# DeltaNet and maxout FFN on one core: beta over the expanded squared norm, the norm on GpSimd, halved transposes, and a PSUM source for the last unit

## The chip, the cores and the metric

The kernel runs on one core of a Trainium2 chip. A core has TensorE (PE in the profile, PEld for its weight loads), VectorE (DVE), ScalarE (ACT), GpSimd (POOL) and SyncE (SP), which only issues DMAs here. ScalarE and GpSimd can issue DMAs as well. Each engine works through its own list of instructions in order, and waits on semaphores for the others. The metric is the device time of one execution in microseconds.

## The reference, cut to what matters

```python
k_n = k / (np.linalg.norm(k, axis=-1, keepdims=True) + 1e-06)
state = np.zeros((B, H, D, D))                      # B, H, S, D = 4, 8, 768, 48
for t in range(S):
    kt, vt, bt = k_n[:, :, t], v[:, :, t], beta[:, :, t, None]
    y[:, :, t] = np.einsum('bhd,bhde->bhe', q[:, :, t], state)
    v_old = np.einsum('bhde,bhd->bhe', state, kt)
    state = state + bt[:, :, :, None] * np.einsum('bhd,bhe->bhde', kt, vt - v_old)
# then x = y as (3072, 384), and
h = np.maximum(np.maximum(x @ w1, x @ w2), x @ w3)  # w1..w3 (384, 768)
out = h @ w_out                                     # w_out (768, 384)
```

The keys stay unnormalised in the kernel. The norm n + 1e-6 enters in two places: beta / (n + 1e-6)^2 scales the key products, and the values are multiplied by n + 1e-6.

## The kernel before, in words

The 768 time steps are cut into 12 chunks of 64. Each chunk is two units (batches with g = 0 and g = 1), and four units make a group, so there are 6 groups (m = 0 to 5). For each unit the keys are transposed on TensorE (`turn`, tile p_t, L345) or with DVE transposes (`turn_blocks`, L396), the products of keys with keys are made (`gram`, p_g, L422) and copied to `at`, with keys against queries in `pt`.

Within a group, each 32 by 32 diagonal block of every unit and head is inverted on VectorE, one block per partition (`solve`). `solve` takes the diagonal of the products (the squared norms), makes the norm, beta over its square, scales the blocks (L560), and eliminates column by column (L574 and L578, two instructions per step). It is a generator: each `yield` ends a portion, and the schedule calls `some(solving, n)` to issue n more portions. For group 0 the blocks come through copies in on-chip memory (`to_blocks`, `first_blocks`), and the inverse goes back by a DVE transpose (L586) and copies (`placed`, L512) into `ut`. For the other groups both ways go through DRAM (`at_d`, `blocks`; `y_d`).

`norms_of` transposes the norms into `nrm`, and `scale` (L303) multiplies the loaded values v_t with them, on GpSimd for all chunks but the last two. Then come, for each chunk: the join of two blocks to 64 (z, j), the product of keys with the state (`old_k`, p_k, subtracted from v_t in L768), the new values (`new`, p_u, L784), the step of the state (`step`, p_s, L814), the output (`to_y`, p_y, L828) and its transpose into `xt`.

The FFN of a group runs while the recurrence of the next one is computed and the blocks of the group after that are solved. There is no automatic schedule: the order of the instructions is the order in which the Python code issues them. The main loop goes through the portions of `ffn(m)` and issues other work behind each: what `LINKS` names for group m + 1, then portions of `solve(m + 2)`:

```python
if i == 8:
    solving = solve(m + 2)
links(m + 1, late.get(m, LINKS).get(i, ""))
...
elif i > 7:
    some(solving, 3 if i > 8 else 1)
```

For m = 1 and 2 portion 8 in `LINKS` is "s0 y0 N2", portions 6 and 7 hold N0 and N1. N is `load_blocks(n)` for a later unit: two memsets and 16 DMA issues, all on GpSimd (L375, L380), since its default queue is GpSimd's. Portion 16 holds P0, a `scale` on GpSimd. In the loop of m = 3 there are no N loads for a group beyond the last.

At the start, loads go out by SP in a fixed order, `turn` and `gram` of the eight first units follow, `solving` is advanced by 1 and then by 17 portions for group 0, and weights are unpacked by ScalarE, VectorE and GpSimd in turn (`weights`, L255 to L270) from pieces that `fetch` loads (w_bits).

Of the kernel before, what the change touches and what calls it, by code (L numbers as in the profile page):

```python
# [14 lines left out]
ALU = mybir.AluOpType  # L15
# [3 lines left out]
BL = 32  # L19
HB = 16  # L20
# [3 lines left out]
def kernel(  # L24
# [31 lines left out]
    nc = tc.nc  # L56

    B, H, S, D = q.shape
# [83 lines left out]
    def load_q(n, queues=one_queue):  # L142
        load(q, qpad[n % NQ], n, queues)
# [128 lines left out]
        )  # L272


    def norm(out, ksum, root, t):

        nc.scalar.sqrt(root, ksum)
        nc.vector.tensor_scalar_max(t, root, 1e-30)
        nc.vector.reciprocal(t, t)
        nc.vector.tensor_tensor(out=t, in0=t, in1=ksum, op=ALU.mult)  # L280
        nc.vector.tensor_tensor(out=t, in0=t, in1=root, op=ALU.add)
        nc.vector.tensor_scalar(
            out=out, in0=t, scalar1=0.5, scalar2=1e-6, op0=ALU.mult, op1=ALU.add
        )

    def small(name, *shape):
        one = name[-1] == "0" or name[-2:] == "bl" or name == "warm"
        return work.tile([128, *shape], FP32, name=name, bufs=2 - one)
# [3 lines left out]
    def norms_of(m, bl):  # L292
        for cc in range(2):
            t = small("nrm", 48)
            for bb in range(2):
                at = 16 * (1 - bb)
                nc.vector.transpose(
                    out=t[rows(bb), at : at + BL], in_=bl[rows(cc)]
                )
            nrms[2 * m + cc] = t[:, 16:32].rearrange("p (g h) -> p g h", g=2)  # L300
# [14 lines left out]
    bl_0 = []  # L315

    def first_norms():
        nc.vector.transpose(out=nrm_0.rearrange("p c g h -> p (c g h)"), in_=bl_0[0])


    kqts, ats, pts, xs, at_d = {}, {}, {}, {}, {}
# [1 line left out]
    def square(name):  # L323
        return work.tile([128, H, C], FP32, name=name, tag="square", bufs=17)

    def by_par(t):
        return t.rearrange("p (j two) x -> p two j x", two=2)
# [83 lines left out]
    def gram(n, parts=(0, 1), queues=one_queue, copy=nc.scalar.copy, later=False):  # L411
        kqt, g = kqts[n], n % 2
        p_g = ps_two("p_g")

        whole = len(parts) == 2 and not g
        for j in range(NP):
            for par in range(2):
                for bb in range(2):
                    kq = kqt[dims(par), j, bb ^ g]
                    for i in (0,) if whole else parts:  # L420
                        c0 = j * 128 + i * C
                        nc.tensor.matmul(  # L422
                            p_g[
                                rows(bb ^ (g * i)), par, c0 : c0 + C * (1 + whole)
                            ],
                            kq[:, 0],
                            kq if whole else kq[:, i],
                        )
        p_v = p_g.rearrange("p two (j i t) -> p two j i t", j=NP, i=2)
        if 1 in parts:  # L430
            pt = pts[n] = square("pt")
            if later:
                return lambda: copy(by_par(pt), p_v[:, :, :, 1])
            else:
                masked(pt, p_v[:, :, :, 1])
        if 0 not in parts:
            return
        at = ats[n] = square("at")
        copy(by_par(at), p_v[:, :, :, 0])  # L439
        if queues:  # L440
            to_dram(n, queues)
# [17 lines left out]
    def in_rows(t):  # L459
        return t.rearrange("p s r -> p (s r)")[:, 0 : BL * BL].rearrange(  # L460
            "p (j i) -> p j i", i=BL
        )
# [5 lines left out]
            "p (s r) -> p s r", s=2  # L468
        )

    def to_blocks(n, engines):


        cc, g = divmod(n, 2)
        for i, engine in enumerate(engines):
            bb, half = divmod(i, 2)
            r, x0 = block(bb, half), 16 * cc + 8 * g
            to = in_rows(in_wo(0))[r, x0 : x0 + H]
            of = ats[n][r, :, BL * half : BL * (half + 1)]
            if engine is nc.scalar:  # L480
                engine.copy(to, of)
            else:
                engine.tensor_copy(to, of)
# [18 lines left out]
        )  # L502


    def placed(cc, i, copy=nc.vector.tensor_copy, xs_of=slice(0, 2 * H)):
        bb, half = divmod(i, 2)
        r = block(bb, half)
        to = ut[cc][r, :, :, BL * half : BL * (half + 1)].rearrange(
            "p g h i -> p (g h) i"
        )  # L510
        of = in_rows(xs[0])[r, :, 16 * cc : 16 * (cc + 1)].rearrange("p i x -> p x i")
        copy(to[:, xs_of], of[:, xs_of])  # L512

    def solve(m):


        x = in_rows(xs[m])
# [7 lines left out]
            nc.gpsimd.memset(y_bl, 0.0)  # L525
        elif m > 2:
            nc.scalar.copy(y, zero.to_broadcast(y.shape))
        bl = small("bl", BL)
        norm(bl, diagonal(x), small("root_bl", BL), small("nt_bl", BL))
        if m == 1:  # L530
            y = ps_two("y_p").rearrange("p b (j i) -> p (b j) i", i=BL)
            nc.scalar.copy(y, zero.to_broadcast(y.shape))
        if m == 2:
            yield
        if m:
            norms_of(m, bl)
            if m == 2:
                yield
            nc.vector.reciprocal(bl, bl)
        else:  # L540
            bl_0.append(bl)
            bl = small("inv_bl", BL)
            nc.vector.reciprocal(bl, bl_0[0])
        nc.vector.tensor_tensor(out=bl, in0=bl, in1=bl, op=ALU.mult)
        nc.vector.tensor_tensor(out=bl, in0=bl, in1=beta_bl[:, m] if m else beta_0, op=ALU.mult)
        if m > 2:
            nc.scalar.copy(diagonal(y), bl)
        else:
            (nc.vector if m == 1 else nc.gpsimd).tensor_copy(diagonal(y), bl)
        if m < FINE:  # L550
            size, xv, yv = HB, in_blocks(xs[m]), in_blocks(y_bl)
            xb = xv[:, :, :, 0:HB]
            by = bl.rearrange("p (s i) -> p s i", i=HB)[:, :, None, :]
            by = by.to_broadcast([128, 2, HB, HB])
        else:
            size, xv, yv = BL, x[:, None], y[:, None]
            xb, by = x, bl[:, None, :].to_broadcast([128, BL, BL])
# [2 lines left out]
        nc.vector.tensor_tensor(out=xb, in0=xb, in1=by, op=ALU.mult)  # L560
        yield
        for j in range(size - 1):
            a, b = j + 1, size - 1 - j
            n = BL // size
            tmp = work.tile([128, 256], FP32, name="tmp", bufs=1)
            t_v = tmp[:, 0 : n * a * b].rearrange("p (s c i) -> p s c i", s=n, i=b)
            row, column, rest = (
                xv[:, :, j, None, j + 1 : size],
                yv[:, :, 0:a, j, None],
                yv[:, :, 0:a, j + 1 : size],  # L570
            )
            if n == 1:
                row, column, rest, t_v = (t[:, 0] for t in (row, column, rest, t_v))
            nc.vector.tensor_tensor(  # L574
                out=t_v, in0=row.to_broadcast(t_v.shape),
                in1=column.to_broadcast(t_v.shape), op=ALU.mult,
            )
            nc.vector.tensor_tensor(out=rest, in0=rest, in1=t_v, op=ALU.subtract)  # L578
            if m == 1 and j == BL - 8:
                nc.scalar.copy(done[:, :, 0:HB], y[:, :, 0:HB])  # L580
            elif m == 1 and j == BL - 2:
                nc.vector.tensor_copy(done[:, :, HB:BL], y[:, :, HB:BL])
            yield
        if m == 0:
            back = in_rows(xs[0])
            nc.vector.transpose(out=back, in_=y.rearrange("p c i -> p i c"))  # L586
            yield
            for i in range(4):
                if i % 2:
                    n = H * (i == 3)  # L590
                    if n:
                        placed(0, i, nc.vector.tensor_copy, slice(0, n))
                    placed(0, i, nc.scalar.copy, slice(n, 2 * H))
                else:
                    placed(0, i, nc.vector.tensor_copy)
            return
        y_d = dram.tile([2, 2, B, H, BL, BL], FP32, name="y_d")
        for cc in range(2):
# [22 lines left out]
    def diagonal(t):  # L621
        return t.rearrange("p j i -> p (j i)")[:, 0 : BL * BL : BL + 1]
# [714 lines left out]
    def keys(n, queues=one_queue, copy=nc.scalar.copy):  # L1337
        gram(n, (0,), queues, copy)
# [5 lines left out]
    load_q(0)  # L1344
    load_k(7)
    load_q(1)
    for _ in range(2):
        fetch(nc.sync)
    load_v(0)
    fetch(nc.sync)  # L1350
    busy(6, ident)
    turn(0, (0,))
    turn(1, (0,), nc.vector.tensor_copy)
    A, V, P = nc.scalar, nc.vector, nc.gpsimd
    keys(0, None)
    to_blocks(0, (P, P, P, P))
    turn(2, (0,))
    keys(1, None, nc.vector.tensor_copy)
    to_blocks(1, (V, V, V, P))
    turn(3, (0,))  # L1360
    keys(2, None)
    to_blocks(2, (A, P, A, P))
    keys(3, None, nc.vector.tensor_copy)
    to_blocks(3, (V, A, V, P))
    first_blocks()
    load_q(2, (nc.gpsimd, nc.gpsimd))
    turn(4, (0,))
    turn(5, (0,))
# [3 lines left out]
    turn(6, (0,))  # L1372
    turn(0, (1,))
    load_q(3, (nc.gpsimd, nc.gpsimd))
    load_beta()
    keys(6)
    gram(0, (1,), None, later=True)()
# [230 lines left out]
```

## Time and profile before

| | us |
|---|---|
| median of three runs | 501.25 (500.38 to 504.06) |
| profiled execution, its own time | 502.97 |
| its span, first to last instruction | 501.3 |
| TensorE busy (share of the span) | 481.9 (96%) |
| VectorE busy | 352.5 (70%) |
| ScalarE busy | 168.5 (34%) |
| GpSimd busy | 189.9 (38%) |

The profile is of one execution. Its span leaves out what lies ahead of the first and behind the last instruction, so its own time is a little longer. Busy shares are averages over stages with different limits; what ends a wait is read from the timelines and from the chain of waits. Times in them are microseconds from the start of the span, and L with a number is a line of the kernel. In a timeline a row is start, busy time, engine, line, operation, written tile and read tiles; the bracket at its end is idle time ahead of it, with what ended it. The mean granted TensorE clock of the execution was 0.973 of full speed.

### The profile page before, as it was taken

To read this page: it belongs to the slowest core of one execution; us is meant where nothing else is said; L and a number is where in the kernel's file an instruction comes from. 1 tells how busy PE (TensorE), PEld (TensorE's weight loads), DVE (VectorE), ACT (ScalarE), POOL (GpSimd) and SP (SyncE) were. 2 spreads that over 40 slices of the span, in tenths; PEclk is the share of its full clock that TensorE was granted. 3 is DMA by queue.
4 is the path that set the end of the run, shared out by engine and by line. 5 is a ranking of instruction groups with operands and counts; after the bars stand their busy time and mean duration, and the time that the engine had idled before them with its cause. 6 is when DMAs were issued, how large, how long until landed. Compare 5 with 4: busy or idle time off the path is not lost.

```text
span 501.3 us, 18765 instructions
## 1 busy us (share of the span) xinstructions
PE 481.9 (96%) x8100; PEld 344.3 (69%) x8100; DVE 352.5 (70%) x830; ACT 168.5 (34%) x323; POOL 189.9 (38%) x313
## 2 busy tenths in 40 slices
PE   7789789999999999999999999999999999999997
PEld 6578578878665555565555565565797457988896
DVE  5888889758697352989552999555998864468763
ACT  4577665976330152200243200252211032212310
POOL 6535683765670394780575870601000020000000
PEclk9758899999999999999999999999999999999999
DMA  8947969775351655543775552834223330330001
GB/s 107 192 73 230 190 174 137 192 195 118 82 144 26 138 123 111 147 123 95 147 137 104 157 139 63 168 57 95 65 63 80 59 76 18 84 80 16 1 16 48
DMA packets 110114, 53.51 MB, mean 107 GB/s; under 512 B 93264, under 2 KB 103920, under 8 KB 110032
## 3 DMA queue, kind: packets, MB, share of 16 engines
q1 hardware_dynamic: 98528, 32.01, 32.4%
q0 software_dynamic: 9088, 19.72, 15.5%
q8 instruction: 64, 1.05, 0.9%
q10 hardware_dynamic: 2416, 0.59, 0.7%
q14 instruction: 18, 0.15, 0.1%
HBM read 39.17 MB, written 13.11 MB: 104 GB/s over the span
## 4 chain that ended last, share of the span: by engine, by line
PE 81%; DVE 7%; DMA 5%; issue 3%; POOL 1%; SPq 1%; ACT 1%; DVEq 0%; POOLq 0%; ACTq 0%
PE p_h L1261 30%; PE p_o L1304 13%; PE p_o L998 10%; PE p_c L1199 4%; PE p_g L422 4%; PE p_u L784 2%; PE p_m L918 2%; PE p_k L756 2%; PE p_y L826 2%; PE p_j L739 2%; PE p_q L756 2%; PE p_t L345 2%; PE p_z L726 2%; PE p_s L807 2%; DMA x_bl<-at_d 1%
## 5 line engine op out<-in xcount | busy, mean ns | idle before, releaser
L1261 PE MATMUL p_h<-xt,w_sb 128*128 128x512 f32 (+1 forms) x468 | 177.9, 524 | 0.8 <-ACT xt L852 0.4
L1261 PEld LDWEIGHTS p_h<-xt,w_sb 128*128 128x128 f32 x468 | 85.3, 191 | 62.4 <-issue 53.2
L1275 DVE TENSOR_TENSOR h<-h,p_h 128x512 f32<-128x512 f32 (+1 forms) x42 | 23.9, 569 | 54.6 <-PE p_h L1261 52.0
L578 DVE TENSOR_TENSOR y_bl<-y_bl,tmp 128x31 f32<-128x31 f32 (+20 forms) x139 | 48.3, 347 | 4.8
L574 DVE TENSOR_TENSOR tmp<-x_bl,y_bl 128x31 f32<-128x31 f32 (+20 forms) x139 | 48.0, 345 | 4.1
L1304 PE MATMUL p_o<-wo_sb,h 128*128 128x384 f32 x144 | 49.2, 490 | 0.4 <-POOL wo_sb L270 0.4
L380 POOL DMA_DIRECT2D turned<-in_q_dram x72 | 39.1, 551 | 4.9 <-POOL turned L375 2.6
L1271 ACT ACTIVATE h<-p_h 128x512 f32<-128x512 f32 (+1 forms) x30 | 16.6, 552 | 70.6 <-PE p_h L1261 70.6
L1304 PEld LDWEIGHTS p_o<-wo_sb,h 128*128 128x128 f32 x144 | 26.8, 190 | 18.5 <-POOL wo_sb L270 1.0
L422 PEld LDWEIGHTS p_g<-kqt 48*64 48x64 f32 x1216 | 25.2, 146 | 10.2 <-issue 7.1
L270 POOL TENSOR_TENSOR w_sb<-mant,up 128x384 int32<-128x384 int32 x18 | 18.9, 1052 | 31.2 <-DVE mant L266 15.1
L422 PE MATMUL p_g<-kqt 48*64 48x64 f32 (+1 forms) x1216 | 28.6, 246 | 0.9 <-ACT kqt L351 0.8
L1310 ACT COPY o_sb<-p_o 128x384 f32<-128x384 f32 x12 | 5.7, 478 | 61.7 <-PE p_o L1304 54.4
L375 POOL MEMSET turned<- 128x96 f32 x18 | 3.3, 189 | 58.9 <-DVE kqt L396 58.9
L611 POOL DMA_DIRECT2D ut<-y_d x4 | 2.6, 650 | 60.3 <-DMA y_d<-y_bl 60.3
L148 POOL DMA_DIRECT2D v_t<-in_v_dram x14 | 11.5, 829 | 28.6 <-PE p_u L784 28.6
L814 DVE TENSOR_TENSOR st<-st,p_s 48x768 f32<-48x768 f32 (+1 forms) x18 | 17.1, 950 | 7.2 <-PE p_s L807 6.6
L1304 PE MATMUL p_o<-w_sb,xt 128*128 128x384 f32 x60 | 21.0, 486 | 0.0
L406 DVE TENSOR_TENSOR pt<-p_g,mask 128x512 f32<-128x512 f32 x20 | 13.7, 689 | 10.3 <-PE p_g L422 10.3
L768 DVE TENSOR_TENSOR v_t<-v_t,p_k 128x768 f32<-128x768 f32 x11 | 10.4, 950 | 13.7 <-PE p_k L756 13.6
L439 ACT COPY at<-p_g 128x512 f32<-128x512 f32 x22 | 12.7, 584 | 18.8 <-DVE pt L406 16.7
L784 PEld LDWEIGHTS p_u<-v_t,ut 64*64 64x64 f32 x768 | 13.4, 142 | 7.7 <-issue 7.7
(247 smaller groups left out, 915.5 us busy)
## 6 DMA issues: line engine op xcount, KB each, us to landing
w_bits<-in_moe_w_dram SPq DMA_DIRECT2D x9, 384.0 KB, 5.6
w_bits<-in_moe_w_dram POOLq DMA_DIRECT2D x9, 384.0 KB, 5.4
turned<-in_q_dram POOLq DMA_DIRECT2D x72, 48.0 KB, 2.7
out_dram<-o_sb SPq DMA_DIRECT2D x34, 96.0 KB, 2.3
y_x<-y SPq DMA_DIRECT2D x32, 96.0 KB, 2.4
qall<-y_x SPq DMA_DIRECT2D x32, 96.0 KB, 2.9
v_t<-in_v_dram POOLq DMA_DIRECT2D x14, 192.0 KB, 4.4
at_d<-at SPq DMA_DIRECT2D x76, 32.0 KB, 2.6
```

Source lines behind the costliest of these rows:

```text
L270: nc.gpsimd.tensor_tensor(out=dst.bitcast(I32), in0=mant_v.bitcast(I32), in1=up_v, op=ALU.add)
L380: (queue, nc.gpsimd)[i].dma_start(out=t[p0 : p0 + 32, bb, at : at + NP * 2 * D].rearrange("p (j x) -> p j x", j=NP), in_=(k, q)[i][2 * bb ...
L422: nc.tensor.matmul(p_g[rows(bb ^ (g * i)), par, c0 : c0 + C * (1 + whole)], kq[:, 0], kq if whole else kq[:, i],)
L574: nc.vector.tensor_tensor(out=t_v, in0=row.to_broadcast(t_v.shape), in1=column.to_broadcast(t_v.shape), op=ALU.mult,)
L578: nc.vector.tensor_tensor(out=rest, in0=rest, in1=t_v, op=ALU.subtract)
L756: nc.tensor.matmul(p_b[rows(bb), par, c0 : c0 + D], kqt[g][dims(par), j, bb ^ g, i], st[dims(par), bb ^ g, g, j],)
L784: nc.tensor.matmul(p_v[rows(bb ^ g), g, i], ut[c % NU][rows(bb), g, h], rhs[rows(bb), g, h],)
L998: nc.tensor.matmul(to[:, g], a[j][:, 128 * g : 128 * (g + 1)], b[j], start=(start and g == of[0] and j == 0), stop=(stop and g == of[-1] a ...
L1199: nc.tensor.matmul(to, w[stays], moves, start=(n == 0), stop=(n == len(terms) - 1))
L1261: nc.tensor.matmul(p_h, w_sb[i][:, t, f * 128 : (f + 1) * 128], xt[:, t, lo : lo + w], start=(t == 0), stop=(t == KT - 1),)
L1275: nc.vector.tensor_tensor(out=h, in0=h, in1=p_h, op=ALU.max)
L1304: nc.tensor.matmul(p_o, stays, moves, start=(n == 0), stop=(n == len(terms) - 1))
```

## The change

The old `norm` computed the root of the squared norm, refined it with a reciprocal, and added 1e-6; then the reciprocal was taken, squared, and multiplied by beta. All but the root ran on VectorE. The new code has two functions. `inverse_square` computes 1 / (s + 2e-6 r + 1e-12) from the squared norm s and the root r, on VectorE. `norm` takes r + 1e-6 and refines it with this inverse in one Newton step, five operations on GpSimd. `solve` calls `norm` behind the copy of the diagonal, and `norms_of` (four DVE transposes per group) is issued behind the first elimination step instead of ahead of the reciprocal.

For group 0, the transpose of the inverse is cut into two halves of 16 columns, and the eight copies into `ut` go to GpSimd, ScalarE and VectorE. The blocks of unit 3 are filled straight from PSUM, and the copy into `at` (on ScalarE now) follows the transpose. Some `to_blocks` copies change engines. `load_v(0)` and two of the first three fetches move in SP's order from ahead of the first `turn` to behind the key products of units 4 and 5.

```diff
-    def norm(out, ksum, root, t):
-
+    EPS = 1e-6
+
+    def inverse_square(out, ksum, root):
         nc.scalar.sqrt(root, ksum)
-        nc.vector.tensor_scalar_max(t, root, 1e-30)
-        nc.vector.reciprocal(t, t)
-        nc.vector.tensor_tensor(out=t, in0=t, in1=ksum, op=ALU.mult)
-        nc.vector.tensor_tensor(out=t, in0=t, in1=root, op=ALU.add)
-        nc.vector.tensor_scalar(
-            out=out, in0=t, scalar1=0.5, scalar2=1e-6, op0=ALU.mult, op1=ALU.add
-        )
+        nc.vector.tensor_scalar_add(out, ksum, EPS * EPS)
+        nc.vector.scalar_tensor_tensor(
+            out=out, in0=root, scalar=2 * EPS, in1=out, op0=ALU.mult, op1=ALU.add
+        )
+        nc.vector.reciprocal(out, out)
+
+    def norm(out, inverse, root):
+        nc.gpsimd.tensor_scalar_add(out, root, EPS)
+        nc.gpsimd.tensor_tensor(out=root, in0=out, in1=out, op=ALU.mult)
+        nc.gpsimd.tensor_tensor(out=root, in0=root, in1=inverse, op=ALU.mult)
+        nc.gpsimd.tensor_scalar(
+            out=root, in0=root, scalar1=-0.5, scalar2=1.5, op0=ALU.mult, op1=ALU.add
+        )
+        nc.gpsimd.tensor_tensor(out=out, in0=out, in1=root, op=ALU.mult)
...
     def first_norms():
-        nc.vector.transpose(out=nrm_0.rearrange("p c g h -> p (c g h)"), in_=bl_0[0])
+        nc.vector.transpose(out=nrm_0.rearrange("p c g h -> p (c g h)"), in_=bl_0.pop())
...
         at = ats[n] = square("at")
+        if later:
+            return p_v[:, :, :, 0], lambda: copy(by_par(at), p_v[:, :, :, 0])
...
-        bl = small("bl", BL)
-        norm(bl, diagonal(x), small("root_bl", BL), small("nt_bl", BL))
+        k_bl, root, nt = small("bl", BL), small("root_bl", BL), small("nt_bl", BL)
+        inverse_square(nt, diagonal(x), root)
...
-        if m:
-            norms_of(m, bl)
-            if m == 2:
-                yield
-            nc.vector.reciprocal(bl, bl)
-        else:
-            bl_0.append(bl)
-            bl = small("inv_bl", BL)
-            nc.vector.reciprocal(bl, bl_0[0])
-        nc.vector.tensor_tensor(out=bl, in0=bl, in1=bl, op=ALU.mult)
-        nc.vector.tensor_tensor(out=bl, in0=bl, in1=beta_bl[:, m] if m else beta_0, op=ALU.mult)
+            yield
+        bl = small("inv_bl", BL)
+        nc.vector.tensor_tensor(out=bl, in0=nt, in1=beta_bl[:, m] if m else beta_0, op=ALU.mult)
         if m > 2:
             nc.scalar.copy(diagonal(y), bl)
         else:
             (nc.vector if m == 1 else nc.gpsimd).tensor_copy(diagonal(y), bl)
+        norm(k_bl, nt, root)
...
         for j in range(size - 1):
+            if m and j == 1:
+                norms_of(m, k_bl)
...
         if m == 0:
-            back = in_rows(xs[0])
-            nc.vector.transpose(out=back, in_=y.rearrange("p c i -> p i c"))
+            bl_0.append(k_bl)
+            back, ahead = in_rows(xs[0]), y.rearrange("p c i -> p i c")
+            A, V, P = nc.scalar.copy, nc.vector.tensor_copy, nc.gpsimd.tensor_copy
+            for part, copies in (
+                (slice(HB, BL), (P, A, P, A)), (slice(0, HB), (V, P, V, A)),
+            ):
+                nc.vector.transpose(out=back[:, part], in_=ahead[:, part])
+                for i, copy in enumerate(copies):
+                    placed(0, i, copy, part)
             yield
-            for i in range(4):
...
-    for _ in range(2):
-        fetch(nc.sync)
-    load_v(0)
     fetch(nc.sync)
...
-    to_blocks(0, (P, P, P, P))
+    to_blocks(0, (P, P, P, None))
     turn(2, (0,))
+    to_blocks(0, (None, None, None, A))
     keys(1, None, nc.vector.tensor_copy)
-    to_blocks(1, (V, V, V, P))
+    to_blocks(1, (V, V, P, P))
     turn(3, (0,))
     keys(2, None)
-    to_blocks(2, (A, P, A, P))
-    keys(3, None, nc.vector.tensor_copy)
-    to_blocks(3, (V, A, V, P))
+    to_blocks(2, (A, P, V, P))
+    products, copied = gram(3, (0,), None, later=True)
+    to_blocks(3, (V, A, V, A), products)
     first_blocks()
+    copied()
...
     load_q(3, (nc.gpsimd, nc.gpsimd))
+    load_v(0)
+    for _ in range(2):
+        fetch(nc.sync)
     load_beta()
```

More of the change, by code (lines that the diff above doesn't have):

```diff
@@ L469, in in_wo, with to_blocks @@
         )
-    def to_blocks(n, engines):
+    def to_blocks(n, engines, of_products=None):
         cc, g = divmod(n, 2)
         for i, engine in enumerate(engines):
+            if engine is None:
+                continue
             bb, half = divmod(i, 2)
@@ L479, in to_blocks @@
             of = ats[n][r, :, BL * half : BL * (half + 1)]
+            if of_products is not None:
+                to = to.rearrange("p (j two) x -> p two j x", two=2)
+                of = of_products[r, :, :, BL * half : BL * (half + 1)]
             if engine is nc.scalar:
@@ L502, in blocks, with placed @@
         )
-    def placed(cc, i, copy=nc.vector.tensor_copy, xs_of=slice(0, 2 * H)):
+    def placed(cc, i, copy=nc.vector.tensor_copy, part=slice(0, BL)):
         bb, half = divmod(i, 2)
@@ L511, in placed @@
         of = in_rows(xs[0])[r, :, 16 * cc : 16 * (cc + 1)].rearrange("p i x -> p x i")
-        copy(to[:, xs_of], of[:, xs_of])
+        copy(to[:, :, part], of[:, :, part])
     def solve(m):
@@ L584, in solve @@
         if m == 0:
-            back = in_rows(xs[0])
-            nc.vector.transpose(out=back, in_=y.rearrange("p c i -> p i c"))
-            yield
-            for i in range(4):
[L589 to L595, printed above, removed]
+            bl_0.append(k_bl)
[7 more added lines that the diff above has]
+                    placed(0, i, copy, part)
+            yield
             return
```

## Prediction

> **What bounds the kernel now.** I read the page first (busy shares, slices, chain), then the chain of waits in order of time, then the timelines of single engines where the change touches them. The page gives TensorE as the bound, with GpSimd far from it:
>
> ```profile
> PE 481.9 (96%) x8100; PEld 344.3 (69%) x8100; DVE 352.5 (70%) x830; ACT 168.5 (34%) x323; POOL 189.9 (38%) x313
> ```
>
> That is an average over two regimes. Until the first hidden-layer matmul (L1261, 44.07 us) the chain runs through VectorE and the inverse of the first group; this is what it shows around the code that the change replaces:
>
> ```profile
> 12.62 1.98 DVE x_bl L487
> 14.63 0.27 ACT root_bl L277
> ...
> 17.00 0.20 DVE inv_bl L545
> 17.25 0.09 issue
> 17.33 0.70 POOL y_bl L549
> ...
> 26.73 1.93 DVE x_bl L586
> 28.69 1.05 ACT ut L512
> 29.76 0.63 ACT ut L512
> 30.39 0.71 DVE t L658
> ```
>
> The reader sees one serial path: transpose, root, norm and reciprocal, elimination, transpose back, copies. From about 69 us on TensorE has no idle time worth naming (stretches 140:165, 165:190 and 300:400 are busy throughout), so there only something that makes TensorE wait counts. The place where the change can do that is the solve for group 3, issued in the ffn loop of group 1. GpSimd there is full of DMA issues, in its timeline:
>
> ```profile
> 203.41 4.33 POOL L380 DMA_DIRECT2D turned<-in_q_dram  x8 [0.29 <-POOL turned L375]
> ...
> 208.22 4.33 POOL L380 DMA_DIRECT2D kmore<-in_k_dram  x8 [0.29 <-POOL kmore L375]
> ...
> 218.66 1.09 POOL L380 DMA_DIRECT2D kmore<-in_q_dram  x2 [1.84 <-issue]
> 219.76 1.49 POOL L303 TENSOR_TENSOR v_t<-v_t,nrm 128x768 f32<-128x768 f32 x1
> ```
>
> and VectorE and TensorE at the same time:
>
> ```profile
> 205.08 0.88 DVE L297 STREAM_TRANSPOSE nrm<-bl 64x32 f32<-64x32 f32 x4
> ...
> 208.79 0.19 DVE L578 TENSOR_TENSOR y_bl<-y_bl,tmp 128x31 f32<-128x31 f32 x1
> 209.02 0.22 DVE L574 TENSOR_TENSOR tmp<-x_bl,y_bl 128x60 f32<-128x60 f32 x1
> ...
> 209.98 0.95 DVE L768 TENSOR_TENSOR v_t<-v_t,p_k 128x768 f32<-128x768 f32 x1
> ```
> ```profile
> 211.49 1.15 PE L784 MATMUL p_u<-v_t,ut 64*64 64x48 f32 x64
> ```
>
> L303 needs the transposed norms of L297, done at 205.96, yet starts at 219.76, directly behind the last DMA issue (0.55 us each): GpSimd takes its instructions in order, and compute waits for the issues ahead of it.
>
> **The change part by part, start-up first.** (1) Last unit from PSUM: VectorE no longer copies p_g into at (0.69, 11.06 to 11.75) before it fills its two blocks. It now does one block of unit 2 and then two from PSUM, nearest row 0.42 (L741, 32x256 from PSUM): 11.33 + 2 x 0.42 = 12.2 against 12.62, a gain of 0.4. The saved copy goes to ScalarE behind the blocks (0.59), before the root, in the 1.34 us in which ScalarE waited there. (2) Inverse: seven operations and their gaps, 14.60 (end of L487) to 17.23 (start of L560), become root 0.26, one addition beside it, one fused 0.21, reciprocal 0.35 (row L279), product 0.19, with gaps 1.2: a gain of 1.4. The elimination then starts at 16.2 instead of 18.06. (3) The norm goes to GpSimd as five dependent operations on 128x32, behind the diagonal copy and ahead of load_q(3) and load_beta. No such row exists. Below: 5 x 0.24, the quiet L549 copy of this size, 1.2 us. Above: 0.29 more each, the wait that the rows show when GpSimd follows its own memset, 2.65 us. I take 2.0, the middle, since the 0.29 belongs to a DMA issue that waits and a wait is there in any case. load_q(3) then is issued by 19.6 instead of 19.3; its landing (4.2 median from GpSimd) is 23.8, and TensorE asks for it at 24.1, so it is covered; uncovered it costs up to 1.2. (4) Transpose in halves: ScalarE sets the pace. Its kqt copy ends at 26.86 behind the weight conversion, whatever VectorE does, so its block copies start at 26.9 instead of 28.69 and take 3 x 0.63 instead of 1.69: the t transposes (30.39) come 1.6 earlier. (5) SP: v_0 and two fetches move behind eight at_d issues (0.70 each, from 16.8): v_0 is issued by 23.7, and lands by 30.1 (6.4 median); its scale starts at 33.1. The next piece of weights lands about 30.5 (5.6), and ScalarE wants it at 30.3: covered to 0.2, and up to 1.6 dearer if it is late. Start-up together: a gain of 1.6, bounds 0 and 2.4 (the upper adds the 0.75 for which p_k waited on st at 52.86).
>
> **The moved norm in the later groups.** The transposes of the norms (four, 0.88) now stand on VectorE behind the first elimination step and wait for the last of the five GpSimd operations. Queued behind them on VectorE: the next steps and the v_t subtraction L768, for which p_u L784 waits on TensorE.
> Group 2: GpSimd is free around 125, VectorE needs the result at 134.8: no wait. Group 1: GpSimd is free from 46.7 to 50.3: none. Group 5: its last DMA issue ends at 342.8 and the reciprocal comes at 350.5: none.
> Group 3: in the loop the DMA issues of load_blocks (N2) precede the first step of the solve, so the five operations stand behind the last kmore issue, which ends at 219.75 (218.66 + 1.09). Then 2.0 for the five, 0.9 for the transposes, and 1.9 for what lay between 209.02 and the end of L768 at 210.93: v_t is ready at 224.6. Before, p_u started at 211.49. Loss 13.1.
> Group 4: the last issue ends at 290.99 (286.66 + 4.33); 291.0 + 2.0 + 0.9 + 1.9 = 295.8 against 285.28. Loss 10.5. GpSimd's v_t load just before (268.33) waited 6.7 us for TensorE, so the two engines keep their distance whatever was lost earlier.
> What VectorE saves in these groups (about 1.2 us each) buys nothing: TensorE was not waiting for it.
> Clock: after the thin stretch 52.1 to 55.4 the granted clock was 0.53 over 55:58.6, and six L1261 matmuls took 2.80 instead of 1.30 to 1.49. Two longer idle stretches cost that once each: 2 x 1.4 = 2.8. Below, 0; above, 4.
> The Trainium skill, "TensorE: Matmul & The Clock Gate" (What's actually happening), says that an idle window of about 3.4 us halves the clock and a busy one restores it. That would be an estimated 1.7 us of lost work per stall, 3.4 in all, and the sum 0.6 higher.
> The Trainium skill, "GPSIMD Engine Reference" (Engine selection), advises against GpSimd for elementwise work, as about twice as slow as VectorE with two inputs. The rows have 1.48 against 0.95 for the same L303 shape. By the page five operations at twice VectorE's 0.19 are an estimated 1.9 us, which leaves the sum as it is: not their length but their place in the queue costs.
>
> **Sum.** -1.6 + 13.1 + 10.5 + 2.8 = +24.8. The profiled execution has a span of 501.3 and its own time 502.97, so 526.1 and 527.8. Its time is 1.7 above the median 501.25; against the median I get 526.0.
>
> **Rivals.**
> No queueing (0.06): GpSimd gets to the norm before N2's issues, VectorE never waits, and only start-up changes: 501.25 - 1.6 = 499.6, not slower. For it: the GpSimd work is only some 2 us in spans of idle. Against: L303 above, held 13.8 us in the same place. It decides if the five operations finish before about 208.8.
> Issues run faster while VectorE is stopped (0.07): the waits between the issues, 2.02 + 0.52 + 1.84 in group 3 and 0.66 + 1.06 in group 4, vanish: 526.0 - 6.1 = 519.9. For it: those are waits for transfers that compete with others. Against: the issues themselves, 0.55 each, are most of the time and stay.
> VectorE is late afterwards (0.07): it resumes 0.5 us further behind than TensorE does in each of the two groups; its 1.62 idle before L828 (219.84) covers this. Without that cover TensorE waits again at h and y, some 3 us a group: 532.
> The inverse as such doesn't get shorter (0.03): late weights or load_q(3) eat the 1.6: 527.6.
> Both stalls as worked out: 0.77.
>
> **How the numbers follow.** Range 517 to 533: below, 519.9 with the upper start-up gain and 2 us less clock loss; above, the late VectorE with start-up gain 0. That leaves out the no-queueing case and little else. A measurement of this kernel can tell about 1% (5 us) from no change. Only the no-queueing case lies within that; a gain over 5 us would need no queueing and a whole start-up at full clock, 0.02. Same 0.04, slower 0.94.
>
> **What would show it.** In the changed profile: the elimination starts near 16.2 and the first L1261 near 42.5; VectorE idle some 14 and 11 us before the transposes of nrm in groups 3 and 4, released by GpSimd; TensorE idle 13 and 10 before p_u; the granted clock low just after; no such wait in groups 1, 2 and 5. It is wrong if GpSimd's five operations in group 3 run before the last kmore issue, or if TensorE does not idle there.

## The result and the profile after

The changed kernel takes 531.09 us in the median (530.22 to 531.73, six runs) against 502.58 us for the kernel before (500.38 to 504.66, six runs): a ratio of 1.0565, 95% interval 1.0531 to 1.0600, or some 28 us slower. The profiled execution has a span of 528.7 us (before 501.3). The forecast was 526.0, within 517 to 533. Some executions of a kernel are over 1.5% longer than its fastest; the ratios here and below leave those out and the medians do not, so a ratio need not be that of two medians.

The page of the changed kernel, its busy times, the granted clock by slices and the group of the transposed norms (busy and mean ns, then idle time ahead and what ended most of it):

```profile
PE 485.0 (92%) x8100; PEld 347.1 (66%) x8100; DVE 346.7 (66%) x805; ACT 169.7 (32%) x326; POOL 200.5 (38%) x345
...
PEclk9759899999999999689999959999999999999999
...
L305 DVE STREAM_TRANSPOSE nrm<-bl 64x32 f32<-64x32 f32 x20 | 4.1, 204 | 27.3 <-POOL bl L292 27.1
```

TensorE's share falls from 96% to 92%, while VectorE has less to do than before (346.7 against 352.5 us) and GpSimd, with 200.5 against 189.9, is busy for only 38% of the span: no engine got more work that would explain 28 us. There are two dips in the clock row past the start, and one group of small transposes has 27 us of idle time ahead of it, ended by GpSimd. The two dips lie at the solves of groups 3 and 4.

Group 3, GpSimd's timeline of the changed kernel (start, busy, engine, line, operation; the bracket is the idle time ahead):

```profile
211.99 3.25 POOL L388 DMA_DIRECT2D kmore<-in_q_dram  x6 [0.29 <-POOL kmore L383]
216.80 1.09 POOL L388 DMA_DIRECT2D kmore<-in_q_dram  x2 [1.55 <-issue]
217.96 0.29 POOL L286 TENSOR_SCALAR bl<-root_bl 128x32 f32<-128x32 f32 x1
...
219.29 0.25 POOL L292 TENSOR_TENSOR bl<-bl,root_bl 128x32 f32<-128x32 f32 x1
220.08 1.47 POOL L311 TENSOR_TENSOR v_t<-v_t,nrm 128x768 f32<-128x768 f32 x1 [0.53 <-DVE nrm L305]
```

VectorE at the same time:

```profile
204.75 0.19 DVE L588 TENSOR_TENSOR y_bl<-y_bl,tmp 128x31 f32<-128x31 f32 x1
219.58 0.88 DVE L305 STREAM_TRANSPOSE nrm<-bl 64x32 f32<-64x32 f32 x4 [14.64 <-POOL bl L292]
220.49 1.14 DVE L584 TENSOR_TENSOR tmp<-x_bl,y_bl 128x60 f32<-128x60 f32 x1
...
222.37 0.95 DVE L777 TENSOR_TENSOR v_t<-v_t,p_k 128x768 f32<-128x768 f32 x1
```

and TensorE, in groups 3 and 4:

```profile
206.67 2.84 PE L1270 MATMUL p_h<-xt,w_sb 128*128 128x512 f32 x6
223.41 1.96 PE L793 MATMUL p_u<-v_t,ut 64*64 64x48 f32 x64 [13.90 <-issue]
225.30 5.50 PE L1313 MATMUL p_o<-wo_sb,h 128*128 128x384 f32 x12
...
310.64 2.07 PE L793 MATMUL p_u<-v_t,ut 64*64 64x48 f32 x64 [11.40 <-issue]
312.64 6.20 PE L1313 MATMUL p_o<-wo_sb,h 128*128 128x384 f32 x12
```

The same p_o in the kernel before, groups 3 and 4:

```profile
212.56 4.14 PE L1304 MATMUL p_o<-wo_sb,h 128*128 128x384 f32 x12
...
286.36 4.14 PE L1304 MATMUL p_o<-wo_sb,h 128*128 128x384 f32 x12
```

The reader sees the chain in three pieces. GpSimd reaches the norm only behind its last kmore issue. VectorE has its inverse and its first elimination step done at 204.94 and then stands for 14.64 us at the transposes. TensorE, with its hidden-layer work done at 209.51, stands for 13.90 us, since the subtraction L777 is queued on VectorE behind those transposes. (TensorE's bracket says "issue" where it names nothing; that L777 is what it waits for follows from the times, its end at 223.32 and p_u at 223.41.) Behind each stall the same matmuls are slow: p_u 1.96 and 2.07 us instead of 1.15, twelve p_o 5.50 and 6.20 instead of 4.14.

The account of the two profiled executions: 13.90 + 11.40 = 25.30 us of stalls; (1.96 - 1.15) + (5.50 - 4.14) = 2.17 and (2.07 - 1.15) + (6.20 - 4.14) = 2.98, together 5.15, of slow matmuls behind them; less 1.98, by which TensorE came earlier to the first stall (209.51 against p_u at 211.49 before); less 0.82, which the last group gives back where the kernel before waits 0.61 us for kmore (at 449.36). That is 27.65 against the 27.4 between the two spans. (Between the medians it is 28.5.)

### The profile page after: what moved, and what is told of

Its sections match the earlier page's. It is cut to its first block, busy times and chain, and to the rows that moved or that the text cites. A ratio compares the mean times of both kernels' runs of the same rounds, so it can differ in the third digit from the quotient of the medians.

```text
span 528.7 us, 18786 instructions
## 1 busy us (share of the span) xinstructions
PE 485.0 (92%) x8100; PEld 347.1 (66%) x8100; DVE 346.7 (66%) x805; ACT 169.7 (32%) x326; POOL 200.5 (38%) x345
## 4 chain that ended last, share of the span: by engine, by line
PE 79%; POOL 7%; issue 4%; DVE 4%; DMA 3%; ACT 2%; SPq 0%; POOLq 0%; DVEq 0%; ACTq 0%
PE p_h L1270 27%; PE p_o L1313 13%; PE p_o L1007 12%; PE p_c L1208 4%; PE p_g L430 4%; POOL kmore L388 3%; PE p_u L793 3%; DMA turned<-in_k_dram 2%; PE p_m L927 2%; PE p_y L835 2%; PE p_k L765 2%; PE p_j L748 2%; PE p_q L765 2%; PE p_z L735 2%; PE p_s L816 2%
## 5 line engine op out<-in xcount | busy, mean ns | idle before, releaser
L1313 PE MATMUL p_o<-wo_sb,h 128*128 128x384 f32 x144 | 52.6, 517 | 0.4 <-POOL wo_sb L270 0.4
L584 DVE TENSOR_TENSOR tmp<-x_bl,y_bl 128x31 f32<-128x31 f32 (+20 forms) x139 | 50.0, 359 | 4.1
L588 DVE TENSOR_TENSOR y_bl<-y_bl,tmp 128x31 f32<-128x31 f32 (+20 forms) x139 | 46.5, 334 | 4.8
L1313 PEld LDWEIGHTS p_o<-wo_sb,h 128*128 128x128 f32 x144 | 28.5, 202 | 20.3 <-issue 3.0
L793 PE MATMUL p_u<-v_t,ut 64*64 64x48 f32 x768 | 16.6, 241 | 26.6 <-issue 26.6
L793 PEld LDWEIGHTS p_u<-v_t,ut 64*64 64x64 f32 x768 | 15.1, 156 | 32.8 <-issue 32.7
L129 POOL DMA_DIRECT2D kpad<-in_k_dram x24 | 16.5, 695 | 21.8 <-PE p_s L816 21.8
L798 ACT COPY u<-p_u 128x768 f32<-128x768 f32 (+1 forms) x12 | 9.2, 771 | 43.8 <-PE p_u L793 43.8
L305 DVE STREAM_TRANSPOSE nrm<-bl 64x32 f32<-64x32 f32 x20 | 4.1, 204 | 27.3 <-POOL bl L292 27.1
```

Source lines behind the costliest of these rows:

```text
L584: nc.vector.tensor_tensor(out=t_v, in0=row.to_broadcast(t_v.shape), in1=column.to_broadcast(t_v.shape), op=ALU.mult,)
L793: nc.tensor.matmul(p_v[rows(bb ^ g), g, i], ut[c % NU][rows(bb), g, h], rhs[rows(bb), g, h],)
L1313: nc.tensor.matmul(p_o, stays, moves, start=(n == 0), stop=(n == len(terms) - 1))
```

## The experiments

The theory is the queue: the norm is late because it stands behind 16 DMA issues, and it costs because urgent work stands behind the waiting transposes. The rivals: GpSimd is too slow for these operations wherever they stand; the start-up edits have a part in the loss; the slow matmuls have another cause than TensorE's idling. Ratios are to the kernel before, measured beside it on the same chip; its medians there were 502.32 (e1 to e4), 503.00 (e5 to e7), 504.35 (e8 to e10) and 503.89 (e11 and e12).

| run | edit | median us | ratio, 95% interval |
|---|---|---|---|
| e1 | N2 behind the norm on GpSimd | 503.34 | 0.9993 (0.9956 to 1.0030) |
| e2 | transposes of the norms later on VectorE | 504.81 | 1.0024 (0.9984 to 1.0064) |
| e3 | norm on VectorE from group 3 on | 503.12 | 1.0019 (0.9984 to 1.0054) |
| e4 | TensorE kept busy through the stalls | 525.63 | 1.0461 (1.0403 to 1.0519) |
| e5 | start-up edits alone | 505.04 | 1.0057 (1.0029 to 1.0084) |
| e6 | new inverse and norm alone | 535.44 | 1.0627 (1.0564 to 1.0690) |
| e7 | norm on VectorE in group 3 only | 514.65 | 1.0238 (1.0179 to 1.0296) |
| e8 | new inverse alone, without the stalls | 503.63 | 0.9991 (0.9956 to 1.0026) |
| e9 | e8 and the halved transpose | 504.15 | 1.0024 (0.9990 to 1.0058) |
| e10 | e3 with the old order on SP | 504.83 | 1.0026 (0.9995 to 1.0057) |
| e11 | the kernel before with one matmul more | 502.57 | 0.9958 (0.9927 to 0.9989) |
| e12 | e3 with the same matmul | 503.33 | 0.9993 (0.9969 to 1.0018) |

**e1: the norm ahead of the issues.**

```diff
-        5: "g2 g3 p1", 6: "u0 N0", 7: "V1 N1", 8: "s0 y0 N2", 9: "x0", 10: "k1 q1",
+        5: "g2 g3 p1", 6: "u0 N0", 7: "V1 N1", 8: "s0 y0", 9: "N2 x0", 10: "k1 q1",
```

> The changed kernel, with the issues of load_blocks N2 one portion later (N2 from portion 8 to portion 9), so that GpSimd does the five norm operations of groups 3 and 4 ahead of those 16 issues. Same instructions on every engine; only GpSimd's order differs. Queue theory (the transposes of the norms wait because the five operations stand behind N2's issues): the stalls of 13.9 and 11.4 us fall below 1 us each, p_u and the 12 p_o matmuls behind it go back to 1.15 and 4.14 us, and the time is 531.1 - 25.3 - 5.2 + 1 = some 501.5. Engine rival (GpSimd is simply the wrong engine for these operations, wherever they stand in its queue): within 2 us of 531. Transfer rival (the 16 transfers land some 2 us later and TensorE waits for kmore instead): 504 to 508.

503.34 us, no difference from the kernel before that 0.4% would show. The same five operations on the same engine cost next to nothing once they stand ahead of the 16 issues. TensorE in e1:

```profile
214.50 1.15 PE L793 MATMUL p_u<-v_t,ut 64*64 64x48 f32 x64 [1.84 <-issue]
215.58 4.14 PE L1313 MATMUL p_o<-wo_sb,h 128*128 128x384 f32 x12
...
288.18 1.15 PE L793 MATMUL p_u<-v_t,ut 64*64 64x48 f32 x64
```

A wait of 1.84 us is left in group 3 (less than 1 was expected), because N1's issues ended at 209.88 in this execution and the norm with them was just late. The engine rival falls, and so does the transfer rival: its trace has no wait of TensorE for kmore behind this place.

**e2: the waiting transposes moved instead.**

```diff
-            if m and j == 1:
+            if m and j == (12 if m > 2 else 1):
                 norms_of(m, k_bl)
```

> The changed kernel, with the four transposes of the norms on VectorE behind elimination step 12 instead of step 1 in groups 3 to 5. GpSimd's queue stays as it is, so the norm is as late as before (about 219.5). Queue theory: nothing urgent stands behind the transposes any more, no stall, some 501 to 502; the scale of v_t on GpSimd starts some 4 us later, which is covered. Engine rival: within 2 us of 531. If the scale or the kpad issues behind it are not covered: up to 4 us more in each group, 509.

504.81 us. The norm is as late as in the changed kernel (GpSimd starts it at 220.34 in group 3), but nothing waits for it any more:

```profile
224.56 0.88 DVE L305 STREAM_TRANSPOSE nrm<-bl 64x32 f32<-64x32 f32 x4
...
213.06 1.15 PE L793 MATMUL p_u<-v_t,ut 64*64 64x48 f32 x64
```

The first line is VectorE's, without a bracket, since it no longer idles there; the second is TensorE's, 11.5 us ahead of those transposes. So it takes both: a late producer, and urgent work queued behind its consumer. Either one alone costs nothing that these runs resolve. The later scale of v_t on GpSimd (225.06) is covered.

**e3: the norm on VectorE.**

```diff
-    def norm(out, inverse, root):
+    def norm(out, inverse, root, engine=nc.gpsimd):
...
-        norm(k_bl, nt, root)
+        norm(k_bl, nt, root, nc.vector if m > 2 else nc.gpsimd)
```

> The changed kernel, with the five norm operations on VectorE in groups 3, 4 and 5 (groups 0 to 2 stay on GpSimd). Queue theory: no wait on GpSimd, five operations of some 0.2 us each more on VectorE, which has room: 501 to 502. Engine rival: the same. Start-up rival (the edits at the start lose time, and the stalls are not all of it): over 504.

503.12 us: the whole loss is gone, and the start-up rival with it, as far as 0.5% can tell. VectorE has the norm done at 206.03 in group 3 and transposes it at 208.01 without a wait.

**e7: one stall at a time.** The same edit for m == 3 alone.

> The changed kernel with the norm on VectorE in group 3 alone. Each stall by itself (theory): group 3 runs through, group 4 still waits about 11.4 us and has its slow p_u and p_o (3.0 more), so some 502.5 + 14.4 = 517. Rival (the stall of group 4 grows or shrinks with the time lost in group 3): 512 or less, or 520 and more.

514.65 us, 1.0238 (9 to 15 us above the kernel before; 14.4 were expected). These are four executions between 512.9 and 517.7, so the time alone would not tell 14.4 from 10. In the profile group 3 runs through, and group 4 stalls:

```profile
293.75 2.07 PE L793 MATMUL p_u<-v_t,ut 64*64 64x48 f32 x64 [10.98 <-issue]
```

Behind it 12 p_o take 5.41: 13.2 us in all. The stall of group 4 does not need that of group 3; the 11.40 us of group 4 are no echo of group 3.

**e4: what the cold clock is worth.** Cold is TensorE at a lower granted clock. The edit adds matmuls of the identity that nobody reads, in chunks 5 and 7 (groups 3 and 4).

```diff
-            p_v = ps_two(name)[:, :, 0 : n * w]
+            whole = ps_two(name)
+            if name == "p_u":
+                for _ in range({5: 52, 7: 42}.get(c, 0)):
+                    nc.tensor.matmul(whole[:, 0, 384:512], ident, ident)
+            p_v = whole[:, :, 0 : n * w]
```

> The changed kernel, with 52 and 42 matmuls of the identity, whose results nobody reads, on TensorE ahead of p_u in groups 3 and 4, so that TensorE works through most of the two stalls. Clock theory (p_u and p_o behind a stall are slow because TensorE had idled): the stalls stay as long as they are, p_u falls from 1.96 and 2.07 to about 1.15, 12 p_o from 5.50 and 6.20 to about 4.14, and the time falls by 5.2 to some 526. Rival (p_o is slow for another reason, its operands or the transfers that run beside it): p_o stays, and the time is 531 or, where the added matmuls outlast the stall, more.

525.63 us, 5.5 less than the changed kernel (5.2 by the two ratios, whose intervals leave some 3 us either way). v_t is ready as late as there: from TensorE's last hidden-layer matmul to p_u it is 14.0 us in group 3 and 10.8 in group 4 (13.90 and 11.40 in the changed kernel). But TensorE comes out of it at full clock:

```profile
210.85 11.77 PE L680 MATMUL p_u<-ident 128*128 128x128 f32 x104
225.02 1.15 PE L797 MATMUL p_u<-v_t,ut 64*64 64x48 f32 x64 [2.40 <-issue]
226.10 4.14 PE L1317 MATMUL p_o<-wo_sb,h 128*128 128x384 f32 x12
```

So the 5.15 us of slow matmuls come from TensorE's own idling: the operands and transfers beside them are the same here. In the changed kernel the stretches (start and end, length, busy time of PE, PEld, DVE, ACT and POOL, then granted clock, share of the DMA engines and GB/s) show it as well:

```profile
209.00:223.40 14.40, 0.51 (x2) 0.02 (x1) 3.63 (x10) 0.00 (x0) 11.61 (x23) 0.69 0.30 77
223.40:225.40 2.00, 1.99 (x65) 1.91 (x65) 1.83 (x7) 0.00 (x0) 0.88 (x2) 0.50 0.54 136
225.40:231.00 5.60, 5.60 (x14) 3.19 (x15) 4.82 (x13) 0.80 (x1) 0.00 (x0) 0.76 0.03 9
```

The granted clock is 0.50 over p_u and 0.76 over the p_o behind it. The Trainium skill, "TensorE: Matmul & The Clock Gate" (What's actually happening), has the clock halved after an idle window of some 3.4 us and restored after a busy one, with windows that run freely. By that page TensorE is slow for one window to two behind a stall, an estimated 1.7 to 3.4 us lost each time. The 2.17 and 2.98 measured agree with it.

**e5 and e6: the two parts of the change by themselves.** e5 is the changed kernel with the old `norm`, e6 the kernel before with the new `inverse_square`, `norm` and the place of `norms_of`.

> The start-up edits alone, on the old norm: unit 3 from PSUM, the block copies on other engines, the transpose in halves, v_0 and two fetches later on SP. The norm and the inverse are those of the kernel before, on VectorE. Theory (the whole loss is in the two stalls, the start-up edits are worth about nothing): the time is within 1.5 us of the kernel before, no stall in groups 3 and 4, first L1270-type matmul between 43.5 and 45. Rival (these edits lose, since v_0 or a piece of weights comes late): 504 to 506. Rival (they bring the 1.6 us that the prediction gave the start-up): 500.7.

> The kernel before with the new inverse and the norm on GpSimd in all groups, and nothing of the start-up edits. Queue theory: both stalls as in the changed kernel, near 13.9 and 11.4 us with a slow p_u and p_o behind each, 530 to 532. Rival (the start-up edits have a part in the loss): below 529.

e6 has the loss (stalls of 13.99 and 11.44 us, p_u 1.96 and 2.14), e5 has no stall. At 535.44 us e6 is above the 530 to 532 that were expected; its profile, which is its slowest execution, starts late, with the first hidden matmul at 46.16 against 44.07. But e5 is not free either: 1.0057, 1.5 to 4.2 us. At the t transposes it is level with the kernel before (30.43 against 30.39), so the start-up edits bring nothing there without the shorter inverse. What it loses comes later: the first hidden matmul is at 45.28, outside the 43.5 to 45 that were expected, and its profile, which is its slowest execution, has 3.90 us of waits within p_k (below). That this is the usual cause was not shown.

**e8, e9, e10: what the start-up edits bring.** e8 is e6 with the norm on VectorE from group 3 on; e9 adds the halved transpose and its copies; e10 is e3 with `load_v(0)` and two fetches back at their old place on SP.

> The kernel before with the new inverse alone: the norm on VectorE in groups 3 to 5 and on GpSimd in groups 0 to 2, no edit of the start-up's order, no halves. Theory (the inverse is 1.4 us shorter at the start; the other start-up edits cost what the run of them alone showed, 2.9 us): 1.4 us below the kernel before, a ratio near 0.997. Rival (what the inverse gains at the start is lost again before TensorE is full): a ratio of 1.000. Rival (the other start-up edits are needed for the gain): 1.000 or above.

> As the run before (new inverse, norm on VectorE from group 3 on, old order of the start-up), and the transpose of the inverse in two halves with its copies on three engines. Theory: the t transposes of VectorE come another 0.3 us earlier (1.47 against 1.74 us from the end of the transpose to them), no more; ratio 0.996 to 0.997. Rival (the halves are what costs in the start-up edits, since GpSimd's copies run beside VectorE): 1.002 or above.

> The changed kernel with the norm on VectorE from group 3 on, and the load of v_0 and the two pieces of weights back at their old, earlier place on SP. Theory (the move of these transfers is what costs): 2 us below the run with the norm on VectorE and the moved transfers, a ratio near 0.997. Rival (the move is covered, as the prediction had it): a ratio near 1.002, like that run.

The times don't tell them apart: none of the three differs from the kernel before. For e8 a gain as large as the expected 1.4 us (0.3%) is not resolved; for e9 and e10 the expected 0.996 to 0.997 lie below the interval, so e10's theory, that the move on SP costs 2 us, falls. The traces tell more. TensorE's last q transposes at the start, in the changed kernel, e8 and e10, one line each:

```profile
22.83 0.66 PE L353 MATMUL p_t<-ident,qall 128*128 128x128 f32 x4
```
```profile
26.80 1.09 PE L353 MATMUL p_t<-ident,qall 128*128 128x128 f32 x4 [4.35 <-DMA qall<-in_q_dram]
```
```profile
28.27 1.09 PE L353 MATMUL p_t<-ident,qall 128*128 128x128 f32 x4 [3.08 <-DMA qall<-in_q_dram]
```

With v_0 and the weights ahead on SP, TensorE waits 3.0 to 4.4 us for q in e8, e9 and e10, though only 1.07 in the profile of the kernel before; with them behind, 0.55 in e2 and not at all in the others. ScalarE's kqt copy comes at 24.88 instead of 27.93 (e8) and 29.39 (e10), and 26.28 in the kernel before. That copy stands ahead of ScalarE's copies of the inverse. So the edits hang together: without SP's new order the halves run into the late kqt copy (e9: 18.32 us from the start of the block transpose to the t transposes, against 17.77 before, 16.84 in e8 and 16.37 to 16.48 in the seven profiles that have all the edits). All of them together win 1.4 us from the block transpose to the t transposes. In e10 that stretch is 16.43 all the same, since its block transpose began 3 us later, at 15.66, and the kqt copy was done by then: a late start hides the wait for q.

**e11 and e12: a pause at the start.** In the profiles so far the block transpose on VectorE begins anywhere from 12.25 to 15.66 us, though the instructions ahead of it are almost the same. TensorE's p_t matmuls differ, 0.66 or 1.11 us, from a pause for the second k tile on. e11 and e12 put a matmul into that pause.

```diff
     turn(0, (0,))
+    busy(1, ident)
     turn(1, (0,), nc.vector.tensor_copy)
```

> The kernel before with one more matmul of the identity between the transposes of the first and the second k tile, where TensorE waits 0.2 to 0.8 us for the tile. In the profiles so far the p_t transposes behind that wait took 0.66 us at once (the changed kernel), from the second on (before), or 1.11 us all the way to 12 us (the run of the norm alone), and the transpose of the blocks began between 12.3 and 15.7 us with it. Theory (it is TensorE's pause there that decides): p_t at 0.66 from about 7 us on, the transpose of the blocks near 12.3, and some 1 us less in the median: ratio 0.998. Rival (something else decides it): no change, ratio 1.000 to 1.001.

> The changed kernel with the norm on VectorE from group 3 on and the same added matmul of the identity. It joins what the runs found: no stall, the short inverse, the q transfers that land early because v_0 is loaded later. Theory: the transpose of the blocks near 12.3, the t transposes near 28.7, first hidden matmul near 42.8, 501 to 501.5 against 503 to 504 for the kernel before: ratio 0.995 to 0.998. Rival (start-up gains are lost again before TensorE is full): 1.000 to 1.002.

TensorE at the start, in e6 (two lines) and in e11:

```profile
6.16 1.08 PE L353 MATMUL p_t<-ident,kpad 128*128 128x128 f32 x4 [0.38 <-DMA kpad<-in_k_dram]
...
8.24 1.11 PE L353 MATMUL p_t<-ident,kpad 128*128 128x128 f32 x4
```
```profile
5.57 0.47 PE L1335 MATMUL p_w<-ident 128*128 128x128 f32 x2
6.17 0.63 PE L345 MATMUL p_t<-ident,kpad 128*128 128x128 f32 x4
```

e11 is 0.42% faster than the kernel before (0.11 to 0.73%), some 2 us, and the only version here that beats it by more than its interval. That the pause is the cause is not shown: one interval in a dozen can miss by chance, and in e11's profile (its slowest execution) the block transpose comes at 12.22, 0.40 us earlier than before, but the first hidden matmul at 44.35, 0.28 later. In e12 the p_t matmuls are fast too (0.63), behind a wait of 0.38 us that was left, but the first hidden matmul is at 43.98 instead of the expected 42.8 and the time is that of the kernel before, 0.9993. Five of the seven profiles of the changed kernel and its variants in e1 to e5 and e7 have fast p_t without the added matmul, so there was little for it to gain there.

## Why the prediction was right, step by step

**Groups 3 and 4, the place and the kind of the wait: right.** The norm behind N2's last issue, VectorE at the transposes, L777 and p_u behind them; no such wait in groups 1, 2 and 5. e1 and e2 show that both halves of this sentence are needed.

**Size of the stalls: 13.1 and 10.5 predicted, 13.90 and 11.40 measured.** The chain of terms was right, and two of them were off in opposite senses. The five operations, put at 2.0 us as the middle of two bounds, took 1.6 (0.22 to 0.29 each, and gaps of 0.07 to 0.09). The work between transposes and v_t, put at 1.9 from the undisturbed steps of before, took 2.86 in group 3: its first tmp took 1.14 us instead of 0.22, beside GpSimd's L311, which the same transposes released. The step that failed is "and 1.9 for what lay between": I took the steps as they were, without asking what else the late transposes would start at that moment.

**Clock: 2.8 predicted, 5.15 measured, and e4 gives some 5.** The mechanism was right, but the size lies outside the prediction's own bounds of 0 to 4. It was taken from the wrong row: the thin stretch at 52.1 to 55.4 us, in which TensorE still worked for 1.08 us, was no measure of an idle stretch of 11 to 14. Nor does the loss grow with the length: the five stalls of the changed kernel, e6 and e7 lost 2.17 to 2.98 us each, and the longest, 13.99 us, lost 2.29.

**Start-up: -1.6 predicted.** The inverse was right (chain from the transpose's end to the scaling 1.17 us, predicted 1.2). The elimination began at 16.58, not 16.2. Unit 3 from PSUM was wrong: the program makes VectorE and ScalarE wait for each other at p_g, so four copies alternate, as the changed kernel's timelines of the two show:

```profile
11.29 0.36 ACT L496 COPY wo_sb<-p_g 32x256 f32<-32x256 f32 x1 [0.36 <-DVE wo_sb L498]
...
11.69 0.42 DVE L498 COPY wo_sb<-p_g 32x256 f32<-32x256 f32 x1 [0.43 <-ACT wo_sb L496]
```

and the transpose begins at 12.62 as before. Even that is luck, since TensorE was earlier in this execution. Its third k tile, before and after:

```profile
7.76 0.66 PE L345 MATMUL p_t<-ident,kpad 128*128 128x128 f32 x4
```
```profile
7.35 0.66 PE L353 MATMUL p_t<-ident,kpad 128*128 128x128 f32 x4
```

From there to the block transpose it is 4.86 us in the kernel before (4.86 to 4.99 in e8, e9 and e11) and 5.27 in the changed one (5.26 to 5.33 in the seven others with these block copies and p_t of 0.66 at this tile). So the edits of the block copies, the PSUM source among them, cost 0.4 us where a gain of 0.4 was predicted. GpSimd's norm costs a little more: the four elimination steps beside it (17.03 to 18.32) take 0.28 to 0.31 us instead of 0.22 to 0.24, 0.27 in all. "ScalarE sets the pace, its kqt copy ends at 26.86 whatever VectorE does" was wrong in its reason: SP's new order, priced at zero, brings q earlier. Two errors nearly cancelled: the t transposes came 1.38 us earlier instead of 1.6 (0.41 from the early tile, less 0.41 for the block copies, 1.48 up to the first elimination step, less 0.27 beside the norm, and 0.17 behind the elimination). But the term as a gain in time was never seen: the first hidden matmul of the seven profiles with this start lies at 42.89 to 44.20 (before 44.07), as the stretch behind the t transposes takes 13.91 to 14.85 us there and took 13.68 before, and without the stalls the kernel is no faster than before (e3, e12). What lengthens that stretch stays open.

**The sum:** +24.8 predicted, +27.4 in span, +28.5 between the medians. The differences in span: stalls +1.7, clock +2.35, the lead at the first stall 1.98 instead of 1.6, and 0.82 given back in the last group. That 531.09 still lies within 517 to 533 is in part luck: the upper end was set by the rival of a late VectorE, which did not happen, and not by longer stalls or a dearer clock.

**The rivals.** No queueing fell with the first trace. Faster issues while VectorE stands fell too: the waits between the issues of N1 and N2 came to 4.4 and 1.7 us in groups 3 and 4 before, and to 4.7 and 1.9 us in the changed kernel, so they are not VectorE's doing. VectorE late afterwards did not happen: from p_u on TensorE is busy throughout, and its distance to before stays at 28.3 us up to 449.

## What to carry to other kernels

Moving work to an idle engine is priced by its place in that engine's queue: look at what stands ahead of it (DMA issues count, 0.55 us each here) and at what stands behind the instruction that will wait for it. Two cures cost nothing that 0.4% would show: issue the producer ahead of the bulk, or move the consumer behind the urgent work. And a stall of TensorE costs more than its length, here 2 to 3 us each in slow matmuls, which idle work in between takes away.

## What the runs showed of the hardware

- A VectorE operation with all operands in SBUF can stand while GpSimd runs a tensor_tensor: the tmp step took 1.14 instead of 0.22 us beside L311 in the changed kernel, in groups 3 and 4 alike, and 1.33 instead of 0.42 beside it in e2. In the kernel before one took 2.46 instead of 0.40 at 290.29, but it began 0.71 us ahead of L303, so that L303 can't be all of its cause. L828 and L814, which read PSUM too, kept their 0.95 us beside L303. The Trainium skill, "Trainium Architecture — The Big Picture" (What this means for kernel authors), calls the port pair that the two share an exclusive lock, not a split of bandwidth; the 1.14 us, which end 0.08 us behind L311, agree.
- Behind a pause of TensorE of 0.2 to 0.9 us at 5.8 us the p_t matmuls take 0.66 us in some profiles and 1.11 in others, in e6 as late as 13.31 us. The length of the pause does not decide it: after 0.20 us they are fast in e4 and slow at first in e5. With the added matmul both profiles have the fast ones, as have six of the twelve without it. The granted clock in the profile does not show it: it is 1.00 over 6 to 13 us in e6, where they are slow, and in e11, where they are fast.
- At one place in TensorE's stream, within p_k near 55 us, it waits for nothing that the profile shows, 0.17 us in e11, 0.77 to 2.96 in most profiles, 3.90 in e5. Such waits are as large as what the start-up edits win; their cause stays open.
